# A list-scheduled kernel planned with other SyncE times, and its layer norms scaled by one two-scalar VectorE op

## The chip, the cores and the metric

The kernel runs on one core of a Trainium2 chip. The metric is the time of one execution on the device in microseconds (us). Each run also lists the span of the core, from its first to its last instruction, and the mean granted TensorE clock (1.0 is full speed). A ratio below 1 means that a kernel is faster than the kernel before. Profiles call TensorE PE (its weight loads PEld), VectorE DVE, ScalarE ACT, GpSimd POOL and SyncE SP; an added q is an engine's queue of instructions.

## The reference, cut to what matters

```python
x = A_x                                                   # 2048 x 512, bf16
x = x + _A_ref(_layernorm(x), mem0, Wq, Wk, Wv, Wo, 32)   # recurrent attention
x = x + _B_ref(_layernorm(x), w_gate, w_up, w_down)       # gated feed-forward, F = 1792
x = x + _A_ref(_layernorm(x), mem0, Wq, Wk, Wv, Wo, 32)   # a second layer, the same weights
x = x + _B_ref(_layernorm(x), w_gate, w_up, w_down)
```

`_A_ref` walks through 64 segments of 32 rows. Each segment attends, in 32 heads of 128, over itself and 8 memory rows, and the output for these 8 rows is the memory of the next segment. So the segments of a layer form a chain. `_layernorm` is `(x - mean) / sqrt(var + 1e-5)`.

## The kernel before

The kernel runs both layers at once, the second six segments behind the first, in 70 steps. Four segments make a block of 128 rows, and feed-forward work of the blocks fills the holes of the attention chain. The V rows of a whole block are computed in one pass, written to a scratch tensor in DRAM by SyncE (SP), and read back per step to other partitions.

The tiles in the profiles below are: `xs` and `xa` the rows before and after attention; `lns` the scalars of a norm and `xn` its result; `xvf`, `xvl` and `hT` their transposes, for the V rows and for the attention; `vst` and `scr` the V rows of a block on their way to DRAM; `sst` the V rows of a step's memory rows (a strip); `vsb` the V rows that a step reads; `pb` the softmax's result; `otsb` the attention's output; `wd` feed-forward weights. `bank` is a PSUM bank.

The order of all instructions is not written by hand. Every piece of work is a task with an engine, a duration and a latency, and a planner of its own makes the order: 24 rounds of a list scheduler, of which the one with the shortest planned span is kept. Only the order reaches the chip. The waits come from semaphores, and the planned times do nothing there.

```python
LAT = {"PE": 205.0, "DVE": 110.0, "ACT": 128.0, "POOL": 40.0, "SP": 4000.0}   # ns
def gap(self, a, b):              # from the end of task a to the start of b, which needs a
    if a.eng == b.eng:
        return a.lat if a.eng[0] in ("DVE", "ACT") or len(a.eng) > 1 else 0.0
    return a.lat + (self.TO_PE if b.eng[0] == "PE" else 0.0)
# ... in the scheduler: a task occupies its engine for its duration
end = now + tk.dur
if self.waits(tk, seen[e]) > 1 and e in ("DVE", "ACT"):
    end += self.WAIT              # 65 ns for a second wait
free[e] = end
# ... the V write of one block, and its read-back, both on SP
pl.add("SP", 450, <write 96 or 32 rows to scr>, lat=4000.0, w=[("vd", j, b, q, kk) ...])
pl.add("SP", 430, <read 24 rows of scr to vsb>, r=[("vd", j, b, q, kk) ...], lat=6000.0)
```

Most copies out of PSUM may go to either ScalarE or VectorE; the planner chooses. The layer norm of 128 rows (79 times in all):

```python
pl.add("DVE", ..., bn_stats);  pl.add("DVE", 100, bn_aggr)
pl.add("DVE", 80, <var + EPS>)
pl.add("POOL", 640, <pow -0.5>)
pl.add("DVE", 80, <bias = -mean * rstd>)
pl.add("ACT", act_ns(D) + 294, <xn = Identity(rstd * x + bias)>)
pl.add("PE", ..., <4 transposes of xn>)
```

Of the kernel before, what the change touches and what calls it, by code (L numbers as in the profile page):

```python
# [11 lines left out]
ACTF = mybir.ActivationFunctionType  # L12
ALU = mybir.AluOpType
# [13 lines left out]
BLK = 4  # L27
# [15 lines left out]
def act_ns(n, psum=False):  # L43
    return n * 0.833 + (52.0 if psum else 110.0)
# [5 lines left out]


class Task:
    __slots__ = ("eng", "dur", "lat", "fn", "deps", "succ", "tail", "boost", "ndep", "ready", "start", "idx", "on", "fresh", "acq", "rel", "durs", "tick", "prev")

    def __init__(self, eng, dur, lat, fn, boost):
        self.durs = dur if isinstance(dur, dict) else {e: dur for e in eng}
        self.eng, self.dur, self.lat, self.fn, self.boost = eng, min(self.durs.values()), lat, fn, boost
        self.deps, self.succ, self.fresh = set(), [], set()
        self.acq, self.rel = [], []
        self.on = None  # L60


class Buf:

    __slots__ = ("pool", "kind", "users", "first", "left", "slot", "t_free", "t_prev")
# [16 lines left out]
class Planner:  # L82
# [43 lines left out]
    def gap(self, a, b):  # L126

        if a.eng == b.eng:
            return a.lat if a.eng[0] in ("DVE", "ACT") or len(a.eng) > 1 else 0.0
        return a.lat + (self.TO_PE if b.eng[0] == "PE" else 0.0)  # L130

    def plan(self, rounds=24):
# [69 lines left out]
    def forward(self):  # L202
# [7 lines left out]
        ready = {e: [] for e in free}  # L210
# [28 lines left out]
        order = []  # L239
        left = len(T)  # L240
        now = 0.0
        seq = {e: 0 for e in free}
        seen = {e: {} for e in free}
        while left:
            while events and events[0][0] <= now:
                _, kind, i = heapq.heappop(events)
                if kind == 0:
                    for e in T[i].eng:
                        heapq.heappush(ready[e], (-T[i].tail, i))
            did = False  # L250
            for e in free:
                if free[e] > now:
                    continue
                h, aside, tk = ready[e], [], None
                while h:
                    q = heapq.heappop(h)
                    if T[q[1]].on is not None:
                        continue
                    if T[q[1]].acq and not fits(T[q[1]], now):
                        aside.append(q)  # L260
                        continue
                    tk = T[q[1]]
                    break
                for q in aside:
                    heapq.heappush(h, q)
                if tk is None:
                    continue
                did = True
                tk.on, tk.start, tk.dur = e, now, tk.durs[e]
                seq[e] += 1  # L270
                tk.tick = seq[e]
                for bf in tk.acq:
                    pool = bf.pool
                    q = min((q for q in pool.free if self.slot_at(q, tk) <= now), key=lambda q: q[0])
                    pool.free.remove(q)
                    bf.slot = q[2]
                    tk.prev += pool.last.get(q[2], [])
                    pool.last[q[2]] = sorted(set(bf.users))
                    pool.used[bf.kind] = pool.used.get(bf.kind, 0) + 1
                end = now + tk.dur  # L280
                if self.waits(tk, seen[e]) > 1 and e in ("DVE", "ACT"):
                    end += self.WAIT
                free[e] = end
                heapq.heappush(events, (end, 1, 0))
                for bf in tk.rel:
                    bf.left -= 1
                    if end >= bf.t_free:
                        bf.t_free, bf.first = end, tk
                    if bf.left == 0:
                        bf.pool.free.append((bf.t_free, bf.first, bf.slot))  # L290
                        bf.pool.used[bf.kind] -= 1
                        heapq.heappush(events, (bf.t_free + bf.first.lat + self.TO_PE, 1, 0))
                        heapq.heappush(events, (bf.t_free + bf.first.lat, 1, 0))
                order.append(tk)
                left -= 1
                for s in tk.succ:
                    n = T[s]
                    n.ready = max(n.ready, end + self.gap(tk, n))
                    n.ndep -= 1
                    if n.ndep == 0:  # L300
                        release(n)
            if not did and left:
                while events and events[0][0] <= now:
                    _, kind, i = heapq.heappop(events)
                    if kind == 0:
                        for e in T[i].eng:
                            heapq.heappush(ready[e], (-T[i].tail, i))
                        did = True
                if did:
                    continue  # L310
                assert events, "no task can go on"
                now = events[0][0]
# [24 lines left out]
class Kern:  # L337
# [176 lines left out]
    def layernorm_T(self, xb, xkey, rw=slice(0, P)):  # L514
        xkeys = xkey if isinstance(xkey, list) else [xkey]
        nc, pl, D, DC = self.nc, self.pl, self.D, self.DC
        i = self.nxt("lns", 3)
        ln = self.lns[i]
        lk = ("lns", i)
        xn = pl.buf(self.xnp)  # L520
        pl.add("DVE", dve_ns(D), lambda: nc.vector.bn_stats(out=ln[rw, 0:6], in_=xb), r=xkeys, w=[lk])
        pl.add("DVE", 100, lambda: nc.vector.bn_aggr(out=ln[rw, 6:8], in_=ln[rw, 0:6]), r=[lk], w=[lk])
        pl.add("DVE", 80, lambda: nc.vector.tensor_scalar(out=ln[rw, 8:9], in0=ln[rw, 7:8], scalar1=EPS, scalar2=None, op0=ALU.add), r=[lk], w=[lk])  # L523
        pl.add("POOL", 640, lambda: nc.gpsimd.tensor_tensor(out=ln[rw, 9:10], in0=ln[rw, 8:9], in1=self.negh[rw, :], op=ALU.pow), r=[lk], w=[lk])  # L524
        pl.add("DVE", 80, lambda: nc.vector.scalar_tensor_tensor(out=ln[rw, 10:11], in0=ln[rw, 6:7], scalar=-1.0, in1=ln[rw, 9:10],
                                                                  op0=ALU.mult, op1=ALU.mult), r=[lk], w=[lk])
        pl.add("ACT", act_ns(D) + 294, lambda: nc.scalar.activation(out=xn[rw, :], in_=xb, func=ACTF.Identity, bias=ln[rw, 10:11], scale=ln[rw, 9:10]),
               r=xkeys + [lk], w=[xn])
        B = pl.buf(self.bank, "bg")

        def pst():
            return B[:, 0:(DC * P) // 2].bitcast(BF16).rearrange("p (c n) -> p c n", c=DC)

        def tr():
            for c in range(DC):
                nc.tensor.transpose(out=pst()[:, c, rw], in_=xn[rw, c * P:(c + 1) * P], identity=self.ident[rw, rw])  # L536

        pl.add("PE", DC * mm_ns(rw.stop - rw.start), tr, r=[xn], w=[B])
        return pst, B
# [16 lines left out]
    def v_pass(self, tile, keys, pieces, boot=False):  # L556
# [3 lines left out]
        for k in range(self.H // 4):  # L560
# [14 lines left out]
            ps = slice((k + 1 - w) * 512, (k + 1) * 512)  # L575
            for c0, j, b, r0, n in pieces:
                d = self.scr[j][b * BLK * XS:(b + 1) * BLK * XS, ps].rearrange("(i r) e -> i r e", i=BLK)[:, r0:r0 + n, :]
                pl.add(("SP", "POOL") if boot else "SP", {"SP": 450, "POOL": 760} if boot else 450,
                       lambda vs=vs, d=d, c0=c0, n=n: ("dma", d, vs[c0:c0 + BLK * n, 0:512 * w]), lat=4000.0 + 500.0 * boot,
                       r=[(vs, q) for q in range(w)] + (["boot"] if boot else []), use=[vs],  # L580
                       w=[("vd", j, b, q, kk) for q in range(r0 // 8, (r0 + n) // 8) for kk in range(k + 1 - w, k + 1)])

    def v_group(self, blocks, psts, boot=False):

# [45 lines left out]
    def emit_step(self, t):  # L630
# [24 lines left out]
        for j in jobs:  # L655
            s = t - j * LAG
            b, i = s // BLK, s % BLK
            row = KOFF if j == 0 else KOFF + L + MEM + SEG - XS
            for k in range(4):
                cs = slice(k * 1024, (k + 1) * 1024)  # L660
                vu = (4 * t + k) % 5
                pl.add("SP", 430, lambda j=j, s=s, row=row, cs=cs, vu=vu: nc.sync.dma_start(
                    out=self.vsb[vu][row:row + XS, :], in_=self.scr[j][s * XS:(s + 1) * XS, cs]),
                    r=[("vd", j, b, q, kk) for q in range(3) for kk in (2 * k, 2 * k + 1)], w=[("vx", j, vu)], lat=6000.0)
        vb = [pl.buf(self.bank), pl.buf(self.bank)]

        def strips():
# [385 lines left out]
```

## Time and profile before

| | before |
|---|---|
| time, median of 3 runs | 1880.26 us |
| TensorE busy | 98% |
| VectorE, ScalarE busy | 68%, 63% |
| streaming time of all matmuls, from their starts | 1761 us |
| lost between the first and the last matmul | 110 us |

TensorE is the bound, and only the last row can be won without less matmul work. The page's chain that ended last, by engine:

```profile
PE 87%; DVE 3%; ACT 2%; DMA 2%; issue 1%; SPq 0%; POOL 0%; ACTq 0%; DVEq 0%; POOLq 0%
```

An engine other than PE in this chain marks stretches in which PE had to wait for it. DMA has 2%.

### The profile page before, as it was taken

The page shows a single profiled execution, that of the slowest core. Times are in us where ns is not written, and L with a number is a line of the kernel's source. Part 1 is how long each engine was busy: PE and PEld are TensorE (multiplying, and loading weights), DVE is VectorE, ACT ScalarE, POOL GpSimd, SP SyncE. Part 2 cuts the span into 40 slices and gives each one's busy share as a digit, 9 for nine tenths or more (in the row PEclk, how much of TensorE's full clock was granted, in tenths as well). Part 3 has the DMA queues.
Part 4 walks back from the last instruction along what each step waited for, and adds up shares of the span by engine and source line. Part 5 has one row for each costly group of instructions (what it writes and reads, how often), then busy time and mean ns, then how long its engine had stood idle before and what let it go on. Part 6 is the DMA issues. An engine that isn't in the chain of part 4 may idle for free.

```text
span 1881.1 us, 94528 instructions
## 1 busy us (share of the span) xinstructions
PE 1838.7 (98%) x41250; PEld 1582.1 (84%) x41250; DVE 1284.4 (68%) x4221; ACT 1176.9 (63%) x2715; POOL 576.9 (31%) x820
## 2 busy tenths in 40 slices
PE   7999999999999999999999999999999999999999
PEld 3578787888988898989888897889888898988787
DVE  5466666776676667766777767666776667766665
ACT  5665566666666666666666666666666666666554
POOL 5422012332423232423323142333323142333312
PEclk9999999999999999999999999999999999999999
DMA  9733334454645454555545354455545364555534
GB/s 352 242 100 108 91 92 120 141 154 129 181 114 163 137 157 118 157 145 153 159 125 159 105 173 130 140 155 153 157 115 162 107 172 119 144 156 142 157 94 145
DMA packets 133890, 273.84 MB, mean 146 GB/s; under 512 B 29147, under 2 KB 65251, under 8 KB 133475
## 3 DMA queue, kind: packets, MB, share of 16 engines
q0 software_dynamic: 58960, 181.47, 32.5%
q1 hardware_dynamic: 74514, 86.32, 16.1%
q8 instruction: 323, 5.29, 1.2%
q14 instruction: 93, 0.75, 0.1%
HBM read 222.04 MB, written 27.26 MB: 133 GB/s over the span
## 4 chain that ended last, share of the span: by engine, by line
PE 87%; DVE 3%; ACT 2%; DMA 2%; issue 1%; SPq 0%; POOL 0%; ACTq 0%; DVEq 0%; POOLq 0%
PE bank L701 32%; PE bank L802 14%; PE bank L901 10%; PE bank L672 7%; PE bank L566 6%; PE bank L925 5%; PE bank L715 5%; PE bank L774 4%; PE bank L785 4%; DMA vsb<-sst 1%; ACT otsb L993 1%; PE bank L536 1%; DMA scr<-vst 1%; DMA vsb<-scr 1%; DVE st L728 1%
## 5 line engine op out<-in xcount | busy, mean ns | idle before, releaser
L701 PE MATMUL bank<-hT,wq_sb 128*128 128x80 bf16 (+1 forms) x8960 | 624.5, 198 | 3.3 <-DVE hT L815 2.2
L701 PE MATMUL bank<-hT,wk_sb 128*128 128x80 bf16 (+1 forms) x8960 | 623.1, 198 | 0.2 <-issue 0.2
L993 ACT CAST qku<-bank 128x480 bf16<-128x480 f32 (+3 forms) x770 | 395.2, 513 | 269.6 <-PE bank L701 253.8
L701 PEld LDWEIGHTS <-wq_sb 128*128 128x128 bf16 x8960 | 458.3, 99 | 26.8 <-issue 6.8
L701 PEld LDWEIGHTS <-wk_sb 128*128 128x128 bf16 x8960 | 450.8, 99 | 0.3 <-issue 0.3
L728 DVE TENSOR_TENSOR st<-bank,maskb 80x240 f32<-80x240 f32 (+1 forms) x732 | 269.5, 369 | 220.5 <-PE bank L715 212.9
L802 PE MATMUL bank<-otsb,wo_sb 128*128 128x80 bf16 (+1 forms) x8960 | 371.4, 198 | 6.9 <-ACT otsb L993 5.3
L802 PEld LDWEIGHTS <-wo_sb 128*128 128x128 bf16 x8960 | 339.2, 99 | 18.8 <-issue 9.4
L893 POOL DMA_DIRECT2D wg<-in_B_w_gate_dram x217 | 165.3, 762 | 494.3 <-PE bank L901 391.9
L993 ACT CAST otsb<-bank 128x480 bf16<-128x480 f32 (+3 forms) x420 | 198.5, 485 | 90.4 <-PE bank L785 78.5
L919 POOL DMA_DIRECT2D wd<-in_B_w_down_dram x217 | 153.9, 711 | 213.2 <-PE bank L785 97.2
L757 DVE TENSOR_TENSOR pb<-st,rz 80x480 bf16<-80x480 f32 x348 | 205.8, 591 | 4.4
L524 POOL TENSOR_TENSOR lns<-lns,negh 128x1 f32<-128x1 f32 (+1 forms) x79 | 46.2, 586 | 492.3 <-DVE lns L523 194.6
L738 ACT ACTIVATE st<-st 80x240 f32<-80x240 f32 (+3 forms) x420 | 160.0, 381 | 47.2 <-DVE st L735 44.3
L740 DVE TENSOR_REDUCE sm<-st 80x6 f32<-80x240 f32 (+3 forms) x420 | 152.2, 363 | 51.6 <-ACT st L738 49.7
L715 PE MATMUL bank<-qku 128*80 128x80 bf16 (+1 forms) x2240 | 176.5, 202 | 0.0
L901 PE MATMUL bank<-xnT,wg 128*128 128x128 bf16 (+2 forms) x1784 | 173.4, 220 | 0.8 <-ACT xnT L993 0.8
L993 ACT CAST ptsb<-bank 128x480 bf16<-128x480 f32 (+3 forms) x295 | 144.2, 497 | 47.2 <-PE bank L774 44.7
L901 PE MATMUL bank<-xnT,wu 128*128 128x128 bf16 (+2 forms) x1784 | 172.4, 219 | 0.0
L715 PEld LDWEIGHTS <-qku 128*80 128x80 bf16 (+1 forms) x2240 | 132.0, 117 | 47.9 <-issue 15.3
L908 DVE SCALAR_TENSOR_TENSOR hff<-th,bank 128x256 bf16<-128x256 f32 (+2 forms) x231 | 94.1, 407 | 104.4 <-ACT th L906 101.9
L894 POOL DMA_DIRECT2D wu<-in_B_w_up_dram x217 | 163.0, 751 | 3.3 <-PE bank L785 1.6
(99 smaller groups left out, 2619.2 us busy)
## 6 DMA issues: line engine op xcount, KB each, us to landing
wg<-in_B_w_gate_dram POOLq DMA_DIRECT2D x220, 256.0 KB, 4.2
wd<-in_B_w_down_dram POOLq DMA_DIRECT2D x219, 256.0 KB, 5.0
wu<-in_B_w_up_dram POOLq DMA_DIRECT2D x217, 256.0 KB, 4.7
vsb<-scr SPq DMA_DIRECT2D x512, 48.0 KB
vsb<-sst SPq DMA_DIRECT2D x280, 64.0 KB
scr<-vst SPq DMA_DIRECT2D x128, 96.0 KB
wv_sb<-in_A_Wv_dram SPq DMA_DIRECT2D x4, 1024.0 KB
wq_sb<-in_A_Wq_dram SPq DMA_DIRECT2D x5, 768.0 KB
```

The source lines that it names most:

```text
L701: nc.tensor.matmul(o_ap, lhsT=W[:, c, h * P:(h + 1) * P], rhs=mv(c), start=(c == 0), stop=(c == DC - 1))
L715: nc.tensor.matmul(s_all(SB)[pr, uh - h0 + i, :], lhsT=qku[:, i, 0, 0:ncol], rhs=qku[:, i, 1, 0:ncol], start=True, stop=True)
L728: pl.add("DVE", dve_ns(n, True), lambda gsz=gsz, hs=hs, st=st, SB=SB, pj_=pj_, npj_=npj_, mk=mk, idx=idx: nc.vector.tensor_tensor(out=st[p ...
L738: pl.add("ACT", act_ns(n), lambda hs=hs, st=st: nc.scalar.activation(out=st[pr, hs], in_=st[pr, hs], func=ACTF.Exp, scale=self.scale), r=s ...
L740: pl.add("DVE", dve_ns(n), lambda hs=hs, st=st, sm=sm: nc.vector.tensor_reduce(out=sm[pr, hs], in_=st[pr, hs], axis=AX.X, op=ALU.add), r=s ...
L757: nc.vector.tensor_tensor(out=o, in0=st[pr, hs].unsqueeze(1).to_broadcast([npart, 2, gsz, L]), in1=rz[pr, :, 0:gsz].unsqueeze(3).to_broadc ...
L802: nc.tensor.matmul(WB[:, c * ncol:(c + 1) * ncol], lhsT=self.wo[:, h, c * P:(c + 1) * P], rhs=otsb[:, hl, 0:ncol], start=(h == 0 and c == ...
L893: pl.add("POOL", 760, lambda wg=wg, fs=fs: nc.gpsimd.dma_start(out=wg[:], in_=self.wgv[:, :, fs]), r=[("wo", self.H - 1)], w=[gk] + bt, la ...
L894: pl.add("POOL", 760, lambda wu=wu, fs=fs: nc.gpsimd.dma_start(out=wu[:], in_=self.wuv[:, :, fs]), r=[("wo", self.H - 1)], w=[uk] + bt, la ...
L901: nc.tensor.matmul(gu[:, 2 * i + k, 0:n], lhsT=W[:, c, i * P:(i + 1) * P], rhs=xnT[:, c, rw], start=(c == 0), stop=(c == DC - 1))
L919: pl.add("POOL", 760, lambda wd=wd, ip=ip: nc.gpsimd.dma_start(out=wd[:], in_=self.wdv[:, 2 * ip:2 * ip + 2, :]), w=[dk] + (["boot"] if se ...
L993: nc.scalar.copy(out=dst, in_=src)
```

## The change

It has two parts. The planner gets other SyncE times: a landing between two SP tasks that depend on each other, a shorter landing of reads and writes, and eight semaphore lanes, so that an SP issue has to wait in the plan until the one eight before has landed. Writes of 32 rows (`n == 8`, 8 rows for each of four segments) hold their lane for 8 us. And the layer norm is scaled by one VectorE op that takes the mean and the reciprocal deviation as per-partition scalars.

```diff
     def gap(self, a, b):
         if a.eng == b.eng:
-            return a.lat if a.eng[0] in ("DVE", "ACT") or len(a.eng) > 1 else 0.0
+            return a.lat if a.eng[0] in ("DVE", "ACT", "SP") or len(a.eng) > 1 else 0.0
@@ forward
+        lanes = []
@@
-                heapq.heappush(events, (end, 1, 0))
+                if e == "SP":
+                    lanes.append(end + tk.land)          # land: 3000 unless set
+                    if len(lanes) >= 8:
+                        free[e] = max(end, lanes[-8])
+                heapq.heappush(events, (free[e], 1, 0))
@@ layernorm_T
-        pl.add("DVE", 80, lambda: nc.vector.scalar_tensor_tensor(out=ln[rw, 10:11], in0=ln[rw, 6:7], scalar=-1.0, in1=ln[rw, 9:10], ...
-        pl.add("ACT", act_ns(D) + 294, lambda: nc.scalar.activation(out=xn[rw, :], in_=xb, func=ACTF.Identity, bias=ln[rw, 10:11], scale=ln[rw, 9:10]),
+        pl.add("DVE", 340, lambda: nc.vector.tensor_scalar(out=xn[rw, :], in0=xb, scalar1=ln[rw, 6:7], scalar2=ln[rw, 9:10], op0=ALU.subtract, op1=ALU.mult),
                r=xkeys + [lk], w=[xn])
@@ v_pass (write)
-   lat=4000.0 + 500.0 * boot
+   lat=3000.0 + 1500.0 * boot
+   if n == 8:
+       tk.land = 8000.0
@@ emit_step (read-back)
-   lat=6000.0
+   lat=5000.0
```

More of the change, by code (lines that the diff above doesn't have):

```diff
@@ L52 @@
 class Task:
-    __slots__ = ("eng", "dur", "lat", "fn", "deps", "succ", "tail", "boost", "ndep", "ready", "start", "idx", "on", "fresh", "acq", "rel", "durs", "tick", "prev")
+    __slots__ = ("eng", "dur", "lat", "fn", "deps", "succ", "tail", "boost", "ndep", "ready", "start", "idx", "on", "fresh", "acq", "rel", "durs", "tick", "prev", "land")
     def __init__(self, eng, dur, lat, fn, boost):
@@ L60, in __init__ @@
         self.on = None
+        self.land = 3000.0
 class Buf:
@@ L524, in layernorm_T @@
         pl.add("POOL", 640, lambda: nc.gpsimd.tensor_tensor(out=ln[rw, 9:10], in0=ln[rw, 8:9], in1=self.negh[rw, :], op=ALU.pow), r=[lk], w=[lk])
-        pl.add("DVE", 80, lambda: nc.vector.scalar_tensor_tensor(out=ln[rw, 10:11], in0=ln[rw, 6:7], scalar=-1.0, in1=ln[rw, 9:10],
-                                                                  op0=ALU.mult, op1=ALU.mult), r=[lk], w=[lk])
-        pl.add("ACT", act_ns(D) + 294, lambda: nc.scalar.activation(out=xn[rw, :], in_=xb, func=ACTF.Identity, bias=ln[rw, 10:11], scale=ln[rw, 9:10]),
+        pl.add("DVE", 340, lambda: nc.vector.tensor_scalar(out=xn[rw, :], in0=xb, scalar1=ln[rw, 6:7], scalar2=ln[rw, 9:10], op0=ALU.subtract, op1=ALU.mult),
                r=xkeys + [lk], w=[xn])
@@ L577, in v_pass @@
                 d = self.scr[j][b * BLK * XS:(b + 1) * BLK * XS, ps].rearrange("(i r) e -> i r e", i=BLK)[:, r0:r0 + n, :]
-                pl.add(("SP", "POOL") if boot else "SP", {"SP": 450, "POOL": 760} if boot else 450,
-                       lambda vs=vs, d=d, c0=c0, n=n: ("dma", d, vs[c0:c0 + BLK * n, 0:512 * w]), lat=4000.0 + 500.0 * boot,
+                tk = pl.add(("SP", "POOL") if boot else "SP", {"SP": 450, "POOL": 760} if boot else 450,
+                       lambda vs=vs, d=d, c0=c0, n=n: ("dma", d, vs[c0:c0 + BLK * n, 0:512 * w]), lat=3000.0 + 1500.0 * boot,
                        r=[(vs, q) for q in range(w)] + (["boot"] if boot else []), use=[vs],
                        w=[("vd", j, b, q, kk) for q in range(r0 // 8, (r0 + n) // 8) for kk in range(k + 1 - w, k + 1)])
+                if n == 8:
+                    tk.land = 8000.0
     def v_group(self, blocks, psts, boot=False):
@@ L663, in emit_step @@
                     out=self.vsb[vu][row:row + XS, :], in_=self.scr[j][s * XS:(s + 1) * XS, cs]),
-                    r=[("vd", j, b, q, kk) for q in range(3) for kk in (2 * k, 2 * k + 1)], w=[("vx", j, vu)], lat=6000.0)
+                    r=[("vd", j, b, q, kk) for q in range(3) for kk in (2 * k, 2 * k + 1)], w=[("vx", j, vu)], lat=5000.0)
         vb = [pl.buf(self.bank), pl.buf(self.bank)]
```

## The prediction

> **What bounds the kernel now.** I began with the page's first two parts, busy time and the 40 slices.
>
> ```profile
> span 1881.1 us, 94528 instructions
> PE 1838.7 (98%) x41250; PEld 1582.1 (84%) x41250; DVE 1284.4 (68%) x4221; ACT 1176.9 (63%) x2715; POOL 576.9 (31%) x820
> ...
> PE   7999999999999999999999999999999999999999
> ```
>
> TensorE is busy from the second slice to the last; VectorE and ScalarE have a third of their time free. Since a busy PE need not be a PE at its peak, I took the starts of all matmuls from the trace. A matmul with 80 columns is followed 36 ns later by the next (27,840 of them), one with 40 after 25 ns (5,760), with 128 after 56 ns (3,912), with 512 after 216 ns (1,261); the 70 strip groups take about 1.7 us each at their best. That makes 1002 + 144 + 219 + 272 + 119 and 5 for odd shapes, 1761 us, which nothing in this change shortens. The first matmul starts 6.4 us into the span and the last one starts 4 us before its end. So 110 us (5.8%) are lost between matmuls. By time: 14 us in the first 100, 17 in the next, 16 from 200 to 400, only 2.8 per 100 us from 400 to 1700 (37), 23 from 1700 on. By size: 18 us are gaps under 60 ns, 42 are 457 gaps of 60 to 125 ns where one kind of matmul follows another, and 50 are 105 gaps above 125 ns, the waits proper. So about 50 us at the very most can be won by scheduling, and 2% is 37.6 us.
>
> Next, the list of who waited for whom, first for PE, then for the SP queue (time in us, times, longest):
>
> ```profile
> PE bank L785 <- DMA vsb<-scr: 6.8, 3, 2.8
> ...
> PE bank L507 <- DVE ident L445: 6.4, 1, 6.4
> ...
> PE bank L536 <- ACT xn L527: 5.8, 5, 3.4
> ```
>
> ```profile
> SPq L682 <- DVE sst L995: 529.6, 57, 16.9
> SPq L662 <- PE bank L785: 358.3, 180, 6.4
> SPq L662 <- DMA scr<-vst: 113.8, 69, 3.3
> ```
>
> The reader should see two waits that the change aims at: PE on the V rows read back from DRAM, and PE on the layer norm's ScalarE op. The other large PE wait, 6.4 us on the identity at the start, is untouched. The SP queue is mostly idle, but 69 times it stands, with everything behind it, until its own write of V rows has landed. The chain that ended last shows this becoming a PE stall; near 319 us:
>
> ```profile
> 319.44 3.69 DMA scr<-vst
> 323.12 0.02 SPq L662
> 323.15 0.03 issue
> 323.18 3.02 DMA vsb<-scr
> 326.20 0.14 issue
> 326.33 0.56 PE bank L785 x6
> ```
>
> Write, landing, read, landing, then the matmul. The same pair stands in the chain near 535, 1170 and 1383 us. In the matmul starts the holes are 2.97 us (323 us), 2.73 (1173), 1.61 (539), with 0.85 + 0.49 (823) and 0.69 (1565) at the same line on DMA in general. That is 9 us.
>
> **What the Trainium skill says.** (1) "TensorE: Matmul & The Clock Gate", section "Back-to-back issue gap", gives N/2.4 + 2.5 ns between matmuls, with a floor of about 25 ns up to 64 columns. The trace agrees: 36, 56, 216 and 25 ns. The same section's slower figures for LDWEIGHTS-MATMUL pairs (81 ns for 128 columns) do not appear here. (2) "DMA: Bandwidth & Descriptors", section "Two DMAs through the same engine are not ordered": the issuing engine has to wait on the first DMA's semaphore before it issues a dependent one. This is what SPq L662 <- DMA scr<-vst shows, and the old plan charged nothing for it (its gap between two tasks of SP was 0). (3) "ScalarE: Activation LUTs", section "What ACT_TABLE_LOAD costs": an ACTIVATE with immediate operands takes 186 ns + 0.833 N, and each pointer operand adds about 93 ns. With two, and N = 512, that is 799 ns; the trace has 814. (4) "VectorE: DVE Perf Modes", section "The perf-mode tier table (the rule you actually need)": tensor_scalar on bf16 in SBUF may run at 4x. From the page's cycle sum, about (512/4 + 150)/0.96 = 290 ns, an estimate. No such op is in this trace; the nearest are the one-element tensor_scalar (144 ns) and the 512-element bf16 copy from PSUM, which the trace has at 408 ns and which is 2x at best. I take 290 to 410 ns, and 0.32 us for the sums.
>
> **The change part by part.** Layer norm: these are its rows in the groups by line.
>
> ```profile
> L527 ACT ACTIVATE xn<-xs,lns 128x512 bf16<-128x512 bf16 x36 | 29.3, 814 | 8.8 <-DVE lns L525 8.0 <-PE bank L536 0.8
> L527 ACT ACTIVATE xn<-xa,lns 128x512 bf16<-128x512 bf16 (+2 forms) x35 | 29.0, 827 | 3.2 <-DVE lns L525 3.1
> ...
> L525 DVE SCALAR_TENSOR_TENSOR lns<-lns 128x1 f32<-128x1 f32 (+1 forms) x79 | 12.0, 153 | 19.9 <-POOL lns L524 19.4
> ```
>
> There are 79 norms. ScalarE loses 79 x 0.82 = 65 us (63% to about 59%). VectorE loses 12 us and gains 79 x 0.32 = 25, so +13 us (68% to 69%). Neither engine bounds the whole. Latency of one norm, from the pow's end to its transposes: 0.15 + 0.82 plus a hop from VectorE to ScalarE (about 0.05 to 0.1) becomes 0.32, so some 0.65 to 0.7 us less. That counts only where PE has nothing else. At the start: PE waits 3.4 us and 1.0 us for the first two norms. The second also waits for the single xn buffer: PE's transposes end at 10.71, ScalarE runs 10.79 to 11.60, PE goes on at 11.66. The first gains 0.65 and the second 0.5 more, so 1.2 us. From 15 to 85 us PE is full and the other boot norms gain nothing. At the end: one or two norms of the last blocks lie in the chain (0.82 us near 1798.5 and one at 1868, the latter beside other matmuls), so 0.7 us. In the middle the other 70-odd norms have matmuls of other steps beside them; PE waited 0.5 us there in all. A freer ScalarE also evicts otsb and qku sooner now and then: 1 us, a guess at the 5.3 us that PE waits for otsb. Sum: 3 us.
>
> SP plan: no instruction is added or removed. The list scheduler now charges 3 us from a V write to its read-back, lowers read landing from 6 to 5 us, and models eight semaphore lanes. Landing measured from the trace's semaphore events (last of an issue's increments, after 200 us): read-back 2.8 us median and 4.9 at the ninth decile; strip copy 2.0; V write 1.9 (96 rows) and 2.1 (8 rows). So write and read-back cost 3 + 5 = 8 us in the plan against 6 before and 4.8 to 8 in the trace: more honest for the pair, and no longer as cautious for the read alone. The lane rule binds rarely. I find issues that start just as the lane eight back lands only eight times, 6.8 us in all, seven of them before 70 us and one of 0.09 us later. There the queue loads weights at the DMA limit (the first slices move 352 and 242 GB/s), so no order can hurry them much. The 8 us lane landing for 8-row writes is far over the measured 2.1 and will push SP issues apart in the plan. As issue order alone reaches the chip, this can only reorder. I expect a better order to remove two thirds of the 9 us: 6 us.
>
> Sum: 1880 - 3 - 6 = 1871. A new plan also moves every evict and matmul; the better half of such moves are kept by the scheduler's own choice among its rounds, so I add 2 us of gain: 1869.
>
> **The rivals.** (a) Moved stall: the VectorE op now stands in front of softmax steps on the engine with the longest chain per step. For it: DVE st waits for nothing but PE in most cases and VectorE has four long ops per head group. Against: 13 us over 79 places is under 0.2 us each. It would make 1872 to 1878. (b) The read's smaller landing (5 instead of 6 us) makes the plan issue later and more reads arrive late: the ninth decile of 4.9 us is just inside. It would add stalls of 1 to 3 us in some of the 16 blocks, and the time would stay at 1880 or rise to 1888. (c) The plan as a whole had been bad at its ends, where 31 of the first 200 us and 23 of the last 181 are lost, and true SP timing repairs these. Half of the 54 would give 1853. Against: PE's waits there are on chains of single-job steps (otsb, st, pb), not on DMA. (d) Nothing: the norm was hidden, the DMA stalls move to other blocks: 1877 to 1881.
>
> **Range and chances.** The sum of named gains is 9 us with 2 for the plan; rivals (a), (b) and (d) lie within 20 us above it, (c) 16 below. Predicted 1869, range 1852 to 1882. Faster by over 2% means under 1842.7 us, three quarters of all that scheduling could win: 4%. Slower by over 2% means over 1917.9, a plan that breaks the steady state: 2%. Within 2%: 94%.
>
> **What would show it.** Right: PE's waits for vsb on DMA fall from 8.6 us to 3 or less, and the write and read-back pair leaves the chain; the first xvf matmul starts near 11.4 instead of 12.6 us; ScalarE falls to about 1112 us and VectorE rises to about 1297; PE's 1761 us of streaming stays, and the loss between matmuls falls from 110 to about 99. The new op shows 0.29 to 0.41 us. Wrong: the op takes 0.5 us or more (no fast mode); the losses of 2.8 per 100 us in the middle move by more than 1; the waits on the V read-back grow; or the gain comes from the first 400 or last 180 us in places that have no norm and no DMA wait.

## The result, and the profile after

A ratio here is the mean time of one kernel's fast runs over that of the other's of the same rounds, so it is not quite the ratio of the medians. At first the changed kernel had a median of 1880.95 us (4 runs) against 1881.7 for the kernel before (4 runs), a ratio of 0.999 (95% interval 0.9968 to 1.0012). With more rounds (e2 below) it was 1878.9 against 1881.18, a ratio of 0.9984 (0.9964 to 1.0004). So it is at most a few us faster, where 11 us were predicted.

The profiled runs differ more, 1874.4 against 1881.1 us of span. First the busy time of the changed kernel:

```profile
span 1874.4 us, 94356 instructions
PE 1835.2 (98%) x41250; PEld 1579.0 (84%) x41250; DVE 1281.1 (68%) x4167; ACT 1137.5 (61%) x2690; POOL 576.2 (31%) x822
...
PE 94%; DMA 1%; ACT 1%; DVE 1%; issue 1%; POOL 1%; SPq 0%; ACTq 0%; POOLq 0%; DVEq 0%
```

The second part of this fence is the chain by engine. PE has gone from 87% to 94% of it and DMA from 2% to 1%. ScalarE lost 39 us and not 65, and VectorE did not gain 13 but lost 3: the planner moved free copies. ScalarE had 1984 copies out of PSUM before and 2038 after, VectorE 301 and 247.

The rows of the norm, in the groups by line (L531 answers to L527 before; out and in, shape, count, busy time, mean ns, idle before and its releasers):

```profile
L531 DVE TENSOR_SCALAR xn<-xs,lns 128x512 bf16<-128x512 bf16 x36 | 14.8, 410 | 27.0 <-POOL lns L530 19.4 <-PE bank L540 7.6
L531 DVE TENSOR_SCALAR xn<-xa,lns 128x512 bf16<-128x512 bf16 (+2 forms) x35 | 14.1, 402 | 5.2 <-POOL lns L530 5.0
```

The op takes 0.41 us, half of the activation's 0.81, but more than the 0.32 that I used. Who PE waited for in the changed kernel:

```profile
PE bank L513 <- DVE ident L451: 6.4, 1, 6.4
PE bank L808 <- ACT otsb L999: 5.4, 16, 0.7
PE bank L540 <- DVE xn L531: 5.2, 7, 2.8
PE bank L707 <- issue: 4.8, 5, 1.9
...
PE bank L791 <- DMA vsb<-sst: 1.9, 2, 1.6
PE bank L791 <- DMA vsb<-scr: 1.9, 1, 1.9
```

And the SP queue, for the same write that made it wait 113.8 us before:

```profile
SPq L668 <- DMA scr<-vst: 13.8, 18, 1.8
```

This is the change at work: SP stands for its own writes 18 times and not 69, and PE waits 3.8 us for `vsb` and not 8.6. In place of those waits stands "issue", holes in which the profile shows nothing to wait for: 4.8 us on L707 and 5.4 us on all lines, against 0.5 us before. The loss between matmuls fell from 109.7 to 103.5 us. Only 1.4 us of that fall lie in PE's waits over 0.15 us, which sum to 35.9 us before and 34.5 after.

One thing makes single runs hard to compare. The clock records of these two traces show stretches of 3.413 us at half speed (in other runs also up to four times as long). Some begin at the end of a hole in PE's work or up to 2.3 us behind it: before at 325.9 us (a hole of 2.97 us from 323.3) and 1175.8 (2.73 us from 1172.9), after at 222.6 (2.08 us from 218.3), 239.7 (1.79 from 238.1) and 1843.9 (2.09 from 1841.4). Others follow shorter holes, as at 1800 us before (0.5 to 0.85 us, three times) and at 145 us (0.5 us, once). And a long hole need not have one: in e1 none follows a hole of 2.85 us near 1175 us. In the control e1 the runs went from 1876.3 us at a clock of 0.999 to 1888.8 at 0.994.

### The profile page after: what moved, and what is told of

Same layout as the page of the kernel before. It is cut to its first block, busy times and chain, and to the rows that moved or that the text cites. A ratio compares the mean times of both kernels' runs of the same rounds, so it can differ in the third digit from the quotient of the medians.

```text
span 1874.4 us, 94356 instructions
## 1 busy us (share of the span) xinstructions
PE 1835.2 (98%) x41250; PEld 1579.0 (84%) x41250; DVE 1281.1 (68%) x4167; ACT 1137.5 (61%) x2690; POOL 576.2 (31%) x822
## 4 chain that ended last, share of the span: by engine, by line
PE 94%; DMA 1%; ACT 1%; DVE 1%; issue 1%; POOL 1%; SPq 0%; ACTq 0%; POOLq 0%; DVEq 0%
PE bank L707 32%; PE bank L808 16%; PE bank L907 11%; PE bank L570 9%; PE bank L678 7%; PE bank L931 5%; PE bank L721 5%; PE bank L780 4%; PE bank L791 4%; PE bank L540 1%; ACT otsb L999 1%; DMA vsb<-sst 0%; PE bank L875 0%; DMA wd<-in_B_w_down_dram 0%; DMA wv_sb<-in_A_Wv_dram 0%
## 5 line engine op out<-in xcount | busy, mean ns | idle before, releaser
L707 PE MATMUL bank<-hT,wq_sb 128*128 128x80 bf16 (+1 forms) x8960 | 625.8, 198 | 5.6 <-issue 2.7
L707 PE MATMUL bank<-hT,wk_sb 128*128 128x80 bf16 (+1 forms) x8960 | 624.3, 198 | 2.1 <-issue 2.1
L707 PEld LDWEIGHTS <-wq_sb 128*128 128x128 bf16 x8960 | 459.1, 100 | 31.3 <-issue 12.0
L707 PEld LDWEIGHTS <-wk_sb 128*128 128x128 bf16 x8960 | 451.7, 99 | 1.2 <-issue 1.2
L999 ACT CAST ptsb<-bank 128x480 bf16<-128x480 f32 (+3 forms) x315 | 155.8, 501 | 65.6 <-PE bank L780 63.2
L741 DVE TENSOR_TENSOR st<-st,mx 80x240 f32<-80x240 f32 (+3 forms) x420 | 155.8, 371 | 3.9
```

Of the source, the lines that this page charges most:

```text
L707: nc.tensor.matmul(o_ap, lhsT=W[:, c, h * P:(h + 1) * P], rhs=mv(c), start=(c == 0), stop=(c == DC - 1))
L741: pl.add("DVE", dve_ns(n), lambda gsz=gsz, hs=hs, st=st, mx=mx: nc.vector.tensor_tensor(out=st[pr, hs], in0=st[pr, hs], in1=mx[pr, hs].uns ...
L999: nc.scalar.copy(out=dst, in_=src)
```

## The experiments

The theory after the first result: the two parts did what they should where they were aimed, and something outside my sum took the gain back. Candidates were a run's accidents (half-speed stretches), one of the two parts itself, or the fact that any edit of the planner's inputs gives a wholly new order.

**e1, the kernel before against itself.** No edit.

> Control: the kernel before once more, against itself. Both theories: ratio 1.000, and the spread of its runs shows how much single runs differ (I expect 1878 to 1885 us) and whether the span goes with the granted clock: in the profiled run before, five half-speed stretches of 3.4 us cost about 8.5 us at a clock of 0.996, so a run at 0.992 should be some 8 us longer than one at 0.996. Span times clock should then be nearly the same in all runs of one kernel, about 1874 us.

Ratio 0.9991 (0.9965 to 1.0017). Span times clock scatters less (standard deviation 1.8 us) than the time (4.8 us) in these six runs; in the 11 runs of the same kernel beside them both scatter by 3.3 us. A difference of 0.2% is therefore at the edge of what six runs can tell. The expectation misread one thing: four half-speed stretches lie inside the span of the profiled run before, up to 6.8 us by their length, and the fifth begins after its end.

**e2, the changed kernel with five rounds.** No edit.

> The changed kernel with more rounds. Theory A (the plan and the norm did win some 6 us of waits, as the two profiles show with 1874.4 against 1881.1 us, and half-speed clock stretches and other accidents of a run hide it): ratio 0.996 to 0.998, span times clock about 1869 us, 5 to 6 us below the control. Theory B (the profiled run was a lucky one and nothing was won): ratio 0.999 to 1.001, span times clock within 2 us of the control.

Ratio 0.9984. The mean clock was 0.9940, against 0.9969 in the 11 runs of the kernel before, and the mean of span times clock 1866.1 against 1874.5. By that the order had won 8 us and more half-speed time had taken 5 back. But in the next session another draw of the same rules (e8) had the clock of the kernel before (0.9938 against 0.9947) and the same ratio, 0.998. So the clock can explain a part of the scatter of runs; that it ate the gain is not shown.

**e3, the norm alone**, with the old planning rules.

```diff
 # kernel before
-        pl.add("DVE", 80, <bias>);  pl.add("ACT", act_ns(D) + 294, <activation>)
+        pl.add("DVE", 340, <tensor_scalar with two per-partition scalars>)
```

> Only the layer norm's two-scalar op, with the old planning rules. If my sum was right about the norm: 3 us faster (ratio 0.998), with the first xvf matmul near 11.6 us in place of 12.6. If the gain is the plan's alone: ratio 0.999 to 1.000 and only about 1 us at the start.

Ratio 0.9968 (0.9949 to 0.9986): 6 us faster, more than the whole change by the means, though the intervals overlap.

**e4, the planning rules alone**, with the old norm ops.

```diff
 # changed kernel
-        pl.add("DVE", 340, <tensor_scalar>)
+        pl.add("DVE", 80, <bias>);  pl.add("ACT", act_ns(D) + 294, <activation>)
```

> Only the planning rules (SyncE landings, lanes), with the old bias op and ScalarE activation. If my sum was right about the plan: 6 us faster (ratio 0.997), PE's waits for vsb on DMA down from 8.6 to 4 us or less. If the plan moves stalls only: ratio 0.999 to 1.001, with the DMA waits gone but the loss between matmuls as large as before (110 us).

Ratio 1.0016 (0.9997 to 1.0035), not faster, though the list of PE's waits has no DMA of `vsb` left. It has 7.7 us for `otsb` instead of 5.3:

```profile
PE bank L810 <- ACT otsb L1001: 7.7, 23, 0.7
```

The second outcome came true, a little above its range: stalls moved.

The parts thus seemed to give -0.32% and +0.16%, and -0.16% together. e5 to e8 asked whether these are properties of the parts.

**e5, the op in the old order.** The planner sees the old tasks; the ScalarE task emits the VectorE op. I compared the emitted streams: TensorE's is identical to that of the kernel before.

```diff
 # kernel before
-        pl.add("DVE", 80, <bias>)
+        pl.add("DVE", 80, lambda: None, r=[lk], w=[lk])
-        pl.add("ACT", act_ns(D) + 294, <activation>)
+        pl.add("ACT", act_ns(D) + 294, <nc.vector.tensor_scalar, two scalars>)
```

> The order of the kernel before is kept instruction for instruction on every engine; only the norm's scaling op runs as the two-scalar op on VectorE in the place that the plan had for the ScalarE op, and the bias op is gone. Theory D (the op itself wins: a shorter norm in front of the V write and its read-back, and a freer ScalarE): ratio 0.997, like the norm alone, and PE's waits for vsb on DMA down from 8.6 us to 4 or less with the old rules. Theory R (the norm-only gain came from being planned anew): ratio 0.999 to 1.001 and the DMA waits stay at 7 us or more; about 1 us less at the start in both.

Ratio 1.0019 (1.0003 to 1.0035), slower, and just above both ranges. First a line from PE's waits in the kernel before, then lines from e5:

```profile
PE bank L774 <- DVE pb L757: 2.5, 10, 0.5
```

```profile
PE bank L784 <- DMA vsb<-scr: 6.2, 3, 2.2
PE bank L773 <- DVE pb L756: 5.1, 13, 0.5
...
PE bank L535 <- DVE xn L526: 3.4, 2, 2.8
PE bank L700 <- DVE hT L814: 3.0, 6, 0.7
PE bank L784 <- DMA vsb<-sst: 2.9, 4, 1.0
```

The norm's own wait fell from 5.8 to 3.4 us. The wait for `pb`, the last VectorE op of the softmax, rose from 2.5 to 5.1, and the waits for `vsb` stayed (9.1 us in all). The test has a flaw at the start. Both theories expected about 1 us less there, but the first `xvf` matmul starts at 13.23 us, against 12.62 before and 11.64 in e3. In the old order the norm's activation was ScalarE's first work, and its function table was loaded at 3.3 us, in idle time. With the activation gone, the load stands in front of the copies that PE waits for (from the timeline of e5):

```profile
11.11 1.28 ACT L992 ACT_TABLE_LOAD   x1 [11.11 <-DVE hT L994]
```

With the start of e3 the ratio would be about 1.001, an estimate from these starts. So, left in the old order, the op did not win, and the 6 us of e3 came with the new order.

**e6, e8: edits that mean next to nothing.** In e6 the norm-only kernel's plan enters the op with its measured 412 ns; in e8 the changed kernel's plan charges 66 ns and not 65 for a second wait.

```diff
-        pl.add("DVE", 340, <tensor_scalar>)     # e6, on e3
+        pl.add("DVE", 412, <tensor_scalar>)
-    WAIT = 65.0                                  # e8, on the changed kernel
+    WAIT = 66.0
```

> The norm-only kernel with one number of the plan changed: the op is entered with the 412 ns that the trace shows and not with 340. Nothing but the order changes. If a new order by itself scatters the time (theory S), this differs from the norm-only kernel by up to 3 us in either direction; if the time follows the rules of the plan and not its accidents (theory P), it is within 1 us of norm-only, ratio 0.996 to 0.997.

> The changed kernel with a number of the plan that means nothing changed (the cost of a second wait 66 ns and not 65). Theory P: within 1 us of the changed kernel, ratio 0.998. Theory S: it moves by 2 to 4 us, so that 0.996 or 1.000 would not surprise, and the differences between the other re-planned kernels of this size say nothing of the rules.

e6 ran at 1.0007 (0.9992 to 1.0022): the 0.3% of e3 were gone, by an edit that changes no instruction, only the order. That is a move of 7 us, more than the 3 that I had allowed for scatter. e8 stayed at 0.998.

**e7, no lanes**, and so no 8 us for small writes. The charge from write to read-back stays.

```diff
 # changed kernel
                     lanes.append(end + tk.land)
-                    if len(lanes) >= 8:
-                        free[e] = max(end, lanes[-8])
```

> The changed kernel without the eight lanes and so without the 8 us landing of small writes; the charge of 3 us from write to read-back stays. Theory P with the lanes as the cause: ratio 0.996 to 0.997, the 3 us that the changed kernel lacks against norm-only come back. If the charge for the landing is the cause: 0.998 as the changed kernel. Under theory S anything from 0.996 to 1.000.

Ratio 0.9884 (0.9868 to 0.9901), a median of 1863.24 us against 1885.5. This beats both kernels, and it lies outside all outcomes that I had named. In its profile 89.3 us are lost between matmuls (109.7 before, 103.5 after). PE waits 2.6 us for `otsb`, and of DMA only the second line is left:

```profile
PE bank L806 <- ACT otsb L997: 2.6, 6, 0.6
PE bank L789 <- DMA vsb<-sst: 2.5, 4, 1.6
```

**e9, e10, e11: more draws.** e9 and e10 are e7 with the two small edits, e11 is e3 with one of them.

```diff
-    WAIT = 65.0                                  # e9, on e7; e11, on e3
+    WAIT = 66.0
-        pl.add("DVE", 340, <tensor_scalar>)     # e10, on e7
+        pl.add("DVE", 412, <tensor_scalar>)
```

> The kernel without lanes (which ran at 0.988 of the kernel before), with the meaningless number of the plan changed (66 for 65 ns). Theory P (the lanes were the cost, the rest of the new rules is good): 0.986 to 0.990 again. Theory S (that kernel drew a lucky order): the time falls back towards the other re-planned kernels, 0.994 to 1.000, and the loss between matmuls from 89 back to 98 us or more.

> The same kernel without lanes, with the norm's op entered at its measured 412 ns. Theory P: 0.986 to 0.990, perhaps a little better as the plan is truer. Theory S: anywhere from 0.988 to 1.001, as the norm-only kernel went from 0.997 to 1.001 by the same edit.

> The norm-only kernel (old planning rules; 0.997 with 340 ns, 1.001 with 412) with 66 for 65 ns. It is a third draw of the same rules. Theory S: 0.995 to 1.001, and the three draws differ by more than their errors of 0.002. Theory P: within 0.001 of 0.997, and the 412 ns kernel is then slower because the longer entry makes a worse plan.

Ratios 0.9952, 0.9922 and 1.0020. The first two fall in the ranges of theory S, the scatter, and the third a little above its. The top of PE's waits in e11, the norm-only kernel planned anew by the old rules:

```profile
PE bank L783 <- DMA vsb<-scr: 15.7, 9, 3.2
PE bank L507 <- DVE ident L445: 6.4, 1, 6.4
```

The read-back alone costs 15.7 us here, where e3, by the same rules and with the same ops, had 1.9. A plan that charges nothing from write to read can only meet the landing by luck.

**e12, lanes with 3 us.**

```diff
 # changed kernel
                 if n == 8:
-                    tk.land = 8000.0
+                    tk.land = 3000.0
```

> The changed kernel with its eight lanes, but small writes land after 3 us in the plan (measured 2.1) and not after 8. Theory P with the 8 us as the fault: like the kernel without lanes, 0.986 to 0.990. If the lanes themselves are the fault: 0.998, as the changed kernel. Theory S: anything from 0.988 to 1.001.

Ratio 0.9890 (0.9866 to 0.9913). The plan is that of e7, task for task on every engine, so the 3 us lanes change nothing, and of the lane rule only the 8 us act. It is also a second measurement of e7's order, in another session: 0.9884 and 0.9890.

**e13, e14, e15: draws to four each.** The changed kernel's rules twice more, the rules without lanes once more.

```diff
-        pl.add("DVE", 340, <tensor_scalar>)     # e13, on the changed kernel
+        pl.add("DVE", 412, <tensor_scalar>)
-    WAIT = 65.0                                  # e14, on the changed kernel; e15, on e7
+    WAIT = 64.0
```

> A third draw of the changed kernel's rules (lanes with the 8 us landing), the norm's op entered at 412 ns. If the 8 us is the cause: 0.996 to 1.001, above all draws or nearly all of the rules without it (0.988, 0.992, 0.995). If it is scatter alone: as likely below 0.994 as above.

> A fourth draw of the same rules, 64 for 65 ns. The 8 us as the cause: 0.996 to 1.001. Scatter alone: as likely below 0.994 as above.

> A fourth draw of the rules without lanes, 64 for 65 ns. The 8 us as the cause: 0.987 to 0.996. Scatter alone: 0.988 to 1.002.

Ratios 0.9907, 1.0023 and 0.9905. e13 missed my range for a harmful 8 us, so the 8 us is no certain loss.

**e16, the old op under the rules without the 8 us**, and **e18, the kernel before planned anew**.

```diff
-                    tk.land = 8000.0             # e16, on e4
+                    tk.land = 3000.0
-    WAIT = 65.0                                  # e18, on the kernel before
+    WAIT = 66.0
```

> The new rules with small writes landing after 3 us (so that no lane binds), but with the old bias op and ScalarE activation. If the norm's op is worth 5 us under the good rules (start 1 us, a freer ScalarE in the middle): 0.991 to 0.996. If the rules do it all: 0.988 to 0.990. If only the two together work: 0.998 to 1.002.

> The kernel before with 66 for 65 ns in its plan: the same work, another order. If re-planning scatters by some 0.3 to 0.5% as with the other rules, 0.995 to 1.006. If the old order was a lucky one: above 1.002; if an ordinary one: near 1.000.

Ratios 0.9990 (0.997 to 1.001) and 1.0022 (0.9994 to 1.005). For e16 that is the third outcome: with the old op even the better rules won nothing, in one draw.

**e17, four forms of the op** in one kernel (wrong results).

```diff
+ four forms in turn: scalars (mean, rstd) | immediates (0.001, 19.5) | one scalar (rstd) | one immediate (19.5)
```

> The changed kernel with the norm's scaling op in four forms in turn: two per-partition scalars (as in the change), two immediates, one per-partition scalar, one immediate. The results are wrong on purpose. If per-partition scalars keep the op out of the 4x mode: about 280 to 320 ns with immediates, 412 with scalars. If the mode is 4x anyway and each scalar costs time: steps, say 280, 345, 412. If tensor_scalar in bf16 runs at 2x here in any form: about 410 ns in all four.

The groups of its profile, one line per form (L532 two scalars, L533 two immediates, L534 one scalar, L535 one immediate):

```profile
L532 DVE TENSOR_SCALAR xn<-xs,lns 128x512 bf16<-128x512 bf16 x11 | 4.5, 412 | 8.7 <-POOL lns L530 7.1 <-PE bank L545 1.6
...
L533 DVE TENSOR_SCALAR xn<-xs 128x512 bf16<-128x512 bf16 x9 | 2.6, 285 | 5.5 <-PE bank L545 5.5
L535 DVE TENSOR_SCALAR xn<-xs 128x512 bf16<-128x512 bf16 x9 | 2.5, 283 | 0.5 <-PE bank L545 0.5
L534 DVE TENSOR_SCALAR xn<-xs,lns 128x512 bf16<-128x512 bf16 x7 | 2.5, 352 | 2.0 <-POOL lns L530 2.0
```

The second outcome came true, as far as durations tell; the trace does not name the mode. My estimate of 290 ns from the page's cycle sum holds for immediates (283 to 285; with the page's 8 cycles of pipe fill, which I left out, it is 298). The first per-partition scalar adds 67 to 69 ns and the second 60. The lines are for rows from `xs`. On rows from `xa` one immediate took 321 ns in the mean, since a few ops of either immediate form take 383 to 405 ns; the medians of the four forms over all rows are 412, 284, 353 and 284.

**All draws together.** The planned span is the planner's own forecast, the span of the round that it kept. It is no time of the chip. The wait is the sum of PE's waits for `vsb` on DMA in that kernel's profile.

| kernel | rules | op | planned span, us | ratio | PE wait for vsb, us |
|---|---|---|---|---|---|
| before | old | old | 1831.9 | 1 | 8.6 |
| e18 | old | old | 1827.3 | 1.0022 | 15.8 |
| e3 | old | new | 1824.8 | 0.9968 | 3.3 |
| e6 | old | new | 1835.0 | 1.0007 | 8.8 |
| e11 | old | new | 1821.8 | 1.0020 | 19.5 |
| e4 | new | old | 1841.4 | 1.0016 | 0.0 |
| e16 | new, no 8 us | old | 1836.8 | 0.9990 | 0.0 |
| e2 (the change) | new | new | 1831.3 | 0.9984 | 4.8 |
| e8 | new | new | 1832.3 | 0.9980 | 4.2 |
| e13 | new | new | 1825.2 | 0.9907 | 3.9 |
| e14 | new | new | 1846.0 | 1.0023 | 3.5 |
| e7 (and e12) | new, no 8 us | new | 1822.1 | 0.9884 (0.9890) | 2.5 (3.3) |
| e9 | new, no 8 us | new | 1830.6 | 0.9952 | 1.6 |
| e10 | new, no 8 us | new | 1825.6 | 0.9922 | 2.7 |
| e15 | new, no 8 us | new | 1820.8 | 0.9905 | 3.3 |

Four things can be read from it. Re-planning by the same rules with the new op scatters the time by 0.5 to 1.2% (the span of each family's ratios), as much as the 0.6% that the change was to have, or more. The wait for `vsb` is 0 to 4.8 us in all ten orders planned by the new rules and 3.3 to 19.5 in the five by the old ones (9.1 in e5). The planned span says nothing of the measured time under the old rules (a correlation of 0.02 over five orders), and orders the kernels almost as the chip does under the new ones (0.95 over ten, with 1.07 us of time for 1 us of plan if a ratio is counted as a part of 1883 us). And the change as delivered was an average draw: its planned span, 1831.3, is that of the kernel before, 1831.9.

The eight lanes with 8 us bind 66 times in the plan of the changed kernel and hold SP for 90 us there, none of it before 190 us. On the chip, seven of its SP issues start just as the lane eight before lands, and all of them are before 70 us. Where the plan waits, the chip does not, and the reverse. The four draws without the 8 us have a mean ratio of 0.992 and the four with it 0.997, with standard deviations of 0.003 and 0.005 within each. That leans to the 8 us being harmful. It does not settle it.

## Why the prediction was right or wrong

**The bound and the size of what can be won: right.** The 1761 us of matmul streaming stayed, and the best order, e7, took 20 us out of the 110, under the 50 that I named as the most. My split of the 110 was less exact. The parts by time add to 107, because the middle holds 39.7 us and not 37. And I did not see that the loss contains the four half-speed stretches, up to 6.8 us.

**The waits that the plan removes: right, and sized nearly right.** I said that PE's waits for `vsb` would fall from 8.6 us to 3 or less, worth 6 us. They fell to 3.8 in the first profile of the changed kernel and 4.8 in the second, and all ten orders by the new rules show the same. The write and read-back pair left the chain as I expected: the chain of the changed kernel has no V write over 0.3 us and one read-back, 2.17 us near 218 us, and SP waits for its writes 13.8 us and not 113.8.

**The norm: the start right, the sum wrong.** The first `xvf` matmul starts at 11.64 us and not 12.62, where I said 11.4. The op was mis-sized, 0.41 us for 0.32; the term is two per-partition scalars, 60 to 69 ns each, which my estimate from the page did not have. I added 0.7 us for the end and 1 us for a freer ScalarE. Neither came: PE's wait for `xn` fell only from 5.8 to 5.2 us, and it waits 5.4 us for `otsb` as before, while the planner refilled the freed ScalarE with 54 more copies. In e5, where nothing was refilled, the wait for `otsb` is 3.9 us. VectorE at 1297 us and ScalarE at 1112 were wrong for the same reason; I had held the choice of engine fixed, and e5, which holds it, has 1302 and 1125. And e5 leans to rival (a): with the order kept, the wait for `pb` grew by 2.6 us and the norm's own shrank by 2.4. The table load at its start keeps this from being a clean test.

**The sum: the step that failed.** It is the end of my working, where I added the terms and then wrote that "the better half of such moves are kept by the scheduler's own choice among its rounds, so I add 2 us of gain". The terms cannot be added when the whole order is drawn anew. The draws of one rule set lie 0.5 to 1.2% apart, 10 to 22 us. The scheduler does keep its best round, but each set of inputs leads its 24 rounds to another end, from 1825.2 to 1846.0 us planned for the changed kernel's rules alone. The change drew a middling one. In the profile pair PE's waits fell by 4.8 us for `vsb` and 0.6 for `xn`, but "issue" grew by 4.9 and a wait for `wd` of 1.3 us came anew, so that almost nothing of what was won is left there. The loss between matmuls fell by 6.2 us all the same: one half-speed stretch fewer is up to 1.7 of it, and the rest lies in gaps under 0.15 us, which I did not follow. In the timed runs only about 3 us remain. What the rest of those runs lost I cannot show, since only the first run of a kernel has a trace.

**The rivals.** (b), more late reads because of the shorter read landing, is spoken against by the ten orders, where PE's waits for `vsb` are short; no run varied that landing alone. (c) put the loss at the ends of the run; e7 won 13 of its 20 us between 400 and 1700 us (39.7 lost before, 26.3 in e7), 6 before 400 and 1 after 1700. (d), that stalls move to other places, is what e4 shows. My range, 1852 to 1882, held the result and the likely class was right; the 11 us were not.

**What stays open.** The "issue" holes. One of about 2 us stands near 1843 us in both profiles of the changed kernel, ones of 1.5 to 2.3 us stand between 1837 and 1860 us in eight other traces, and e7 has none. The order alone does not decide it: e12, in the order of e7, has 2.2 us of "issue", and e1 has 2.2 where the same kernel had 0.5. The traces say more, in the queue that carries instructions (this line is the same in the pages before and after):

```profile
q8 instruction: 323, 5.29, 1.2%
```

These are 323 packets of 16 KB, one for every 256 of the 82,762 instructions that PE's records have after. Ten traces have all matmuls. In them 12 of the 13 "issue" holes over 0.7 us stand at the same place of the count of 256, give or take one. The instruction at that place never starts sooner than 1.20 us after the end of its packet, in any of the ten, while the one before it starts up to 1 us ahead of that end. So, by these traces, the holes are waits of PE for its own next instructions. What makes a packet late, and whether a plan can avoid it, no run shows. Also open: whether the 8 us harms in the mean, and why the new rules with the old op did not win. e4 and e16 have no `vsb` wait left and 7.7 and 6.8 us for `otsb`, so a fuller ScalarE is a possible cause, argued and not shown; e9, with the new op, waits 8.9 us for `otsb` and is faster all the same.

## What to carry to other kernels

Where a planner or compiler makes the order, a kernel's time is a draw: re-plan with inputs that mean nothing, see how far the time moves, and count no part's gain that is smaller than this. Look at the planner's own forecast before the chip: here it was 1831.3 us for the changed kernel against 1831.9, no gain. Two sets of rules do not forecast by the same measure, but these numbers could have been had before the prediction. A truer model of waits may pay less by the one order that it gives than by making that forecast worth trusting. Then many draws can be made without the chip and the one with the best forecast kept; e7 and e15 suggest this, but no run chose an order by its forecast in advance. And an engine that is relieved does not stay relieved when the planner may refill it.

## What the Trainium skill lacked or had wrong

- "DVE: scalar operands, raw-bit mode, write accounting and state across instructions", section "1. Scalar operands", does not say what a pointer scalar costs. Here a bf16 tensor_scalar of 128x512 took 285 ns with immediates, 352 with one fp32 pointer scalar and 412 with two.
- "TensorE: Matmul & The Clock Gate", section "What's actually happening", ties the half-speed state to an idle window of about 3.4 us. The stretches here have that length (3.413 us, or a multiple) but five in the two profiles followed holes of 1.8 to 3.0 us, shorter than the window.
- "Runtime: NRT & Kernel Launch", section "Instruction fetch mechanics", has no number for a wait of TensorE on its own instructions in code without branches. Here such holes over 0.7 us took up to 2.1 us each and 3.8 us of one run, and two runs of one order had them in part at other places (967, 1179 and 1841 us; 1390 and 1846 us).
